# Zero padding moved from the K stacks to the Q stacks in a fused attention and GEGLU layer, with units reordered and new priorities

## The chip, the cores and the metric

One core of one Trainium2 chip runs the kernel. The metric is the device time of one launch in microseconds (us); the profile is of one execution of the same program. About 1% is what a timing of this kernel can tell from no change.

## The reference

One transformer layer over 2048 tokens of width 512, in fp32: pre-layer-norm attention with a compressive memory, then a pre-layer-norm GEGLU feed-forward, each with its residual.

```python
H = 32; Dh = 16; N = 4; L = 512              # heads, head width, segments, segment length
q, k, v = (split_heads(layernorm(x) @ w) for w in (wq, wk, wv))
for s in range(N):
    logits = qs @ ks.T * Dh ** -0.5 + mask   # causal inside the segment
    a_dot  = softmax(logits) @ vs
    pq     = phi(qs)                         # t + 1 where t > 0, else exp(t)
    a_mem  = (pq @ M) / (pq @ z + 1e-6)
    o      = g * a_mem + (1 - g) * a_dot     # g = sigmoid(beta), one per head
    M += phi(ks).T @ vs;  z += sum(phi(ks))
h  = x + concat(o) @ wo
h2 = h + (gelu(layernorm(h) @ w_gate) * (layernorm(h) @ w_up)) @ w_down   # 1376 hidden columns
```

## The kernel before

**Precision.** Most products are kept near fp32 by splitting operands into a high and a low fp32r part and adding three matmuls (high by high, high by low, low by high). For the attention logits the same three products sit in one matmul: a head's 16 dimensions are stacked four times in 64 partitions (high, low, high, and a row that carries a constant on the K side and the row maximum on the Q side). Two heads share the 128 partitions.

**Stacks.** Projections of q and k are written to `hl` tiles (high and low part, 128 partitions x 512 queries). Transfers issued by SP (L694 for Q, L700 for K) copy them, SBUF to SBUF, into the stacks `stq` and `stk`. Since two heads share the partitions, one operand must hold zeros where the other head lies. Before the change this is K: `stk` is `[128, 2, 2, 512]`, with one plane per head `a`, half of it zero, and `stq` is `[128, 2, 512]`.

**Units and halves.** The 32 heads are four chunks `c` of eight heads; a unit is a chunk in one segment `s` (`UNITS`, sixteen of them), and a half `Q` is four heads of a unit, two pairs `p` of two heads `a`. For each half:

- `pass_a` computes logits with queries as output rows (PE, L796), and DVE takes their negated masked row maxima with one reduction each (L806, `nm`). The maxima are split into high and low (L822, L825, `mm`), transposed (PE, L829), copied to `mx` (L832) and sent by a transfer into a free row of the Q stack (L834). Only keys up to the end of a block of 128 queries are computed.
- `pass_b` computes the logits again with keys as rows, in four key blocks `kb` of 128 (PE, L868, and L861 for `kb` 3), now with the maximum subtracted by the extra row. ACT takes exp (L875), GpSimd zeroes the upper triangle (L878), and `accum` multiplies by V with a column of ones for the sum (PE, L899, four heads side by side in 32-column tiles). For `kb` 3, GpSimd first adds the two K planes (`k3`, L846) and ACT spreads the Q stack over two planes (`q3`, L850), so that one matmul of 256 columns serves two heads.
- `mem` computes the memory part (L755, L771). `wo_seg` multiplies by `wo` (L972) and adds the residual; `ln2` normalizes (DVE, L561), transposes (PE, L578) and forms operands of the feed-forward, which is a Strassen-like product (`ffn`, L1144) and `down` (L1205).

**What sets the order.** The program is straight-line. A list scheduler (`Sched`) fixes the order of every engine's queue ahead of time: among the operations that could start within a small window of the earliest, it takes the one with the lowest priority number. A priority is the place in the program plus an offset from the table `DUE`, by kind of work (`q`, `k`, `d` for stack transfers, `v`, `m`, `a`, `b`, `p`, `o`, `w` for `wo`, `l` for the first layer norm) and by unit or half. Tiles come from pools (`Pool_`) that hand out buffers in order and pass them on to a later stage when they retire. The eight PSUM banks are three for projections and the like, two for `pass_a`, two for `pass_b`, one for `accum`.

Of the kernel before, what the change touches and what calls it, by code (L numbers as in the profile page):

```python
# [7 lines left out]
F32 = mybir.dt.float32  # L8
# [7 lines left out]
P = 128  # L16
# [12 lines left out]
UNITS = [(c, s) for h in range(2) for c in range(NCH) for s in (2 * h, 2 * h + 1)]  # L29
# [211 lines left out]
def infini_geglu(ctx: ExitStack, tc: tile.TileContext, x, wq, wk, wv, wo, beta,  # L241
# [56 lines left out]
    stk_t = many("stk", 4, [P, 2, 2, D], F32R)  # L298
    PSK = Pool_(stk_t, fifo=True, then=Parts(2, *[PBL] * 5, *[FIN] * 3))
    stq_t = slots("stq", 4)  # L300
    PSQ = Pool_(stq_t, fifo=True, then=Parts(1, PBL, PBL, Parts(2, *[PHH] * 2), Parts(2, *[PHH] * 2)))

    k3_t = many("k3", 1, [P, 2, P], F32R)
    q3_t = many("q3", 2, [P, 2, 2, P], F32R)
    PK3, PQ3 = Pool_(k3_t, fifo=True), Pool_(q3_t, fifo=True)
# [23 lines left out]
    PNM = Pool_(many("nm", 2, [P, 2, 2, 4]))  # L329
    PMM = Pool_(many("mm", 2, [P, 2, 2, 8], F32R))  # L330
    PMX = Pool_(many("mx", 2, [32, P]))
# [7 lines left out]
    one = sb("one", [P, 1])  # L339
    gt = sb("gt", [P, 2, NCH])  # L340
# [46 lines left out]
    vz3 = [Val() for _ in q3_t]  # L387
    vone, vq0, vk0, vv0 = Val(), [Val() for _ in stq_t], [Val() for _ in stk_t], [Val() for _ in va_t]

# [5 lines left out]
    def c_fill():  # L395
        for i, t in enumerate(stq_t):
            pool(0.93, -4.2 + 0.1 * i + (i > 1), lambda t=t: nc.gpsimd.memset(t.bitcast(F32), 0.0),
                 [vcalm[0]] if i > 1 else [], [vq0[i]])
        for i, t in enumerate(q3_t):
            pool(0.5, -3.8 + 0.1 * i, lambda t=t: nc.gpsimd.memset(t.bitcast(F32), 0.0),  # L400
                 [vcalm[0]], [vz3[i]])
        for i, t in enumerate(va_t):
            def ones(t=t):
                nc.gpsimd.memset(t[:, :, 16:136:17], 1.0)
                nc.gpsimd.memset(t[:, :, 136:152], 1.0)
            pool(0.25, -3.5 + 0.1 * i, ones, [vcalm[0]], [vv0[i]])

        def c_amask():
            nc.gpsimd.memset(amask, 0.0)
            nc.gpsimd.affine_select(amask[:, 3 * P:], amask[:, 3 * P:], pattern=[[-1, P]],  # L410
                                    compare_op=OP.is_ge, fill=NEG, base=0, channel_multiplier=1)
        pool(1.0, -3, c_amask, [vcalm[0]], [vamask])

    def c_stk(i, after):
        t = stk_t[i]
        for a in range(2):
            own, other = slice(64 * a, 64 * a + 64), slice(64 - 64 * a, 128 - 64 * a)
            act(2 * D, -4.2 + i, lambda a=a, own=own: nc.scalar.activation(
                t[own, :, a], one[own, :, None].to_broadcast([64, 2, D]), AF.Copy),
                [vone] + after, [vk0[i]], src=0.1, chain=True)  # L420
            pool(0.93, -4.2 + i, lambda a=a, other=other: nc.gpsimd.memset(
                t[other, :, a].bitcast(F32), 0.0), after, [vk0[i]], chain=True)


# [239 lines left out]
    def qkv(U):  # L664
# [8 lines left out]
        for i in range(2):  # L673
# [14 lines left out]
            for h, Q in enumerate(half):  # L688
                dst = (STQ, STK)[i][Q]
                zeros = (vq0, vk0)[i][Q:Q + 1]  # L690
                for r, part in enumerate(((0, 1, 0), (0, 0, 1))[i]):
                    if i == 0:
# [5 lines left out]
                    for a in range(2):  # L698
                        dma(moved + 0.2 + h, lambda dst=dst, r=r, part=part, h=h, hl=hl, a=a:
                            nc.sync.dma_start(  # L700
                                dst.t[64 * a + r:64 * a + 64:4, :, a].bitcast(F32),
                                hl.t[64 * h + 32 * a:64 * h + 32 * a + 32, part].bitcast(F32)),
                            [hl] + zeros, [dst], kb=64, chain=True)
                if i == 0 and Q >= len(stq_t):
                    dma(moved + 0.2 + h, lambda dst=dst: nc.sync.dma_start(
                        dst.t[3:P:32].bitcast(F32), amask[0:16, 0:2 * P]), [vamask], [dst],
                        kb=16, chain=True)
# [74 lines left out]
    def pass_a(Q):  # L782
# [4 lines left out]
        def part(heads, i):  # L787

            w = (i + 1) * P
# [513 lines left out]
```

## Time and profile before

| | us |
|---|---|
| median of three timed runs | 839.55 |
| lowest and highest | 834.55, 841.9 |
| span of the profiled execution | 837.1 |
| TensorE (PE) busy | 812.1 (97%) |
| VectorE (DVE) busy | 613.4 (73%) |
| ScalarE (ACT) busy | 540.6 (65%) |
| GpSimd (POOL) busy | 505.3 (60%) |
| TensorE matmuls | 4709 |

The span runs from the first to the last instruction of the profiled execution; its own launch time was not recorded apart, and the span lies inside the range of the timed runs. Busy time of PE includes modelled ends of pipelined matmuls, so an engine shown busy can still run below its pace. Attention fills the first 476 us or so, the feed-forward the rest.

### The profile page before, as it was taken

The numbers are of one execution on the slowest core, as the hardware profiler recorded it, in microseconds if no ns is written. First come the engines' busy times: TensorE is split into PE (matmuls) and PEld (weight loads), VectorE is DVE, ScalarE is ACT, GpSimd is POOL, SyncE is SP. The second block draws the span as 40 slices with busy tenths as digits, with TensorE's granted clock in tenths as the row PEclk, the third lists the DMA queues.
The fourth block names the chain that finished last, engine by engine and source line by source line (L and its number), as shares of the span: only waits on it lengthen the run. The fifth ranks groups of instructions, "written<-read, shape, count | busy, mean of one in ns | idle before, by whom it ended". The sixth has DMA issues, their size and how long they took to land.

```text
span 837.1 us, 15362 instructions
## 1 busy us (share of the span) xinstructions
PE 812.1 (97%) x4709; PEld 627.1 (75%) x4709; DVE 613.4 (73%) x1831; ACT 540.6 (65%) x1063; POOL 505.3 (60%) x751
## 2 busy tenths in 40 slices
PE   5999999999999999999999899999999999999998
PEld 4777787777767877677756588778788887788886
DVE  7888876797887887789686783677457956656565
ACT  6877778688876757776575662687467554545551
POOL 7534445544444645546755695788787676778750
PEclk9999999999999999999999799999999999999999
DMA  6643545636436554565554465531211251212102
GB/s 230 160 111 94 162 108 164 172 103 195 123 104 172 165 158 129 152 177 141 165 168 144 142 219 158 189 100 52 63 51 42 83 181 43 63 46 64 51 1 100
DMA packets 71750, 103.52 MB, mean 124 GB/s; under 512 B 14324, under 2 KB 24884, under 8 KB 71668
## 3 DMA queue, kind: packets, MB, share of 16 engines
q1 hardware_dynamic: 71668, 102.54, 42.1%
q8 instruction: 37, 0.61, 0.3%
q14 instruction: 45, 0.37, 0.1%
HBM read 54.92 MB, written 21.43 MB: 91 GB/s over the span
## 4 chain that ended last, share of the span: by engine, by line
PE 76%; DVE 11%; ACT 4%; DMA 3%; issue 3%; POOL 3%; SPq 1%; POOLq 0%; ACTq 0%; DVEq 0%
PE bank L1144 20%; PE bank L1205 13%; PE bank L899 8%; PE bank L796 7%; PE bank L618 7%; PE bank L868 6%; PE bank L972 5%; DVE junk L806 4%; PE bank L647 3%; PE bank L578 1%; POOL raw L1121 1%; PE bank L771 1%; PE bank L725 1%; DMA cd<-pv_dram 1%; DVE row L561 1%
## 5 line engine op out<-in xcount | busy, mean ns | idle before, releaser
L806 DVE CUSTOM_DVE_ANT_0 junk<-bank,amask 128x256 f32<-128x256 f32 (+3 forms) x512 | 228.2, 485 | 43.0 <-PE bank L796 39.4
L875 ACT ACTIVATE pt<-bank 128x512 f32<-128x512 f32 (+1 forms) x352 | 181.3, 559 | 53.9 <-PE bank L868 42.4
L878 POOL TENSOR_SCALAR_AFFINE_SELECT pt<-pt 128x128 f32<-128x128 f32 (+2 forms) x352 | 118.5, 347 | 155.3 <-ACT pt L875 151.0
L796 PE MATMUL bank<-stk,stq 128*128 128x512 f32 (+2 forms) x384 | 126.9, 377 | 3.7 <-DVE nm L806 2.1
L868 PE MATMUL bank<-stq,stk 128*128 128x384 f32 (+2 forms) x384 | 114.1, 356 | 2.9 <-ACT pt L875 2.3
L618 PE MATMUL bank<-xt,w 128*128 128x512 f32 x384 | 108.6, 395 | 1.2 <-DVE xt L588 1.1
L1210 DVE TENSOR_TENSOR pt<-pt,bank 128x512 f32<-128x512 f32 x96 | 64.9, 685 | 40.2 <-PE bank L1205 39.9
L796 PEld LDWEIGHTS bank<-stk,stq 128*128 128x128 f32 x384 | 68.4, 188 | 25.8 <-DVE nm L806 11.4
L868 PEld LDWEIGHTS bank<-stq,stk 128*128 128x128 f32 x384 | 67.1, 188 | 21.8 <-ACT pt L875 10.3
L618 PEld LDWEIGHTS bank<-xt,w 128*128 128x128 f32 x384 | 69.9, 188 | 12.6 <-DVE xt L588 1.6
L899 PE MATMUL bank<-pt,vaug 128*32 128x512 f32 (+3 forms) x1024 | 79.1, 445 | 0.0
L899 PEld LDWEIGHTS bank<-pt,vaug 128*32 128x32 f32 x1024 | 29.6, 111 | 41.0 <-issue 31.4
L647 PE MATMUL bank<-wv,xt 128*128 128x256 f32 x384 | 54.9, 283 | 0.1
L1144 PE MATMUL bank<-xt,w 128*128 128x512 f32 (+1 forms) x201 | 54.3, 391 | 0.0
L647 PEld LDWEIGHTS bank<-wv,xt 128*128 128x128 f32 x384 | 52.3, 190 | 2.2 <-DVE pq L630 0.4
L434 POOL TENSOR_TENSOR w<-raw,w 128x512 fp32r<-128x512 f32 x24 | 30.9, 1289 | 30.8 <-ACT w L429 27.6
L1114 POOL TENSOR_TENSOR w<-raw,w 128x512 fp32r<-128x512 f32 (+3 forms) x36 | 41.7, 1160 | 2.8 <-ACT w L1112 2.6
L1144 PEld LDWEIGHTS bank<-xt,w 128*128 128x128 f32 (+1 forms) x201 | 37.1, 186 | 8.3 <-ACT junk L1151 0.2
L806 DVE DVE_READ_ACCUMULATOR2_ANT nm<- 128x1 f32 x512 | 42.0, 82 | 0.0
L1144 PE MATMUL bank<-stk,w 128*128 128x512 f32 (+1 forms) x135 | 38.0, 390 | 0.3 <-DVE vaug L1156 0.3
L920 ACT ACTIVATE pvs<-bank 128x512 f32<-128x512 f32 x32 | 19.2, 599 | 28.6 <-PE bank L899 14.8
L1121 POOL TENSOR_TENSOR raw<-raw,raw 128x256 f32<-128x256 f32 (+1 forms) x44 | 35.8, 813 | 3.0
(299 smaller groups left out, 1805.5 us busy)
## 6 DMA issues: line engine op xcount, KB each, us to landing
stq<-hl SPq DMA_DIRECT2D x96, 128.0 KB
stk<-hl SPq DMA_DIRECT2D x192, 64.0 KB
pv_dram<-pvs SPq DMA_DIRECT2D x32, 256.0 KB
r<-r_dram SPq DMA_DIRECT2D x28, 256.0 KB
row<-x SPq DMA_DIRECT2D x24, 256.0 KB
raw<-wg SPq DMA_DIRECT2D x20, 256.0 KB
raw<-wu SPq DMA_DIRECT2D x20, 256.0 KB
raw<-wd SPq DMA_DIRECT2D x20, 256.0 KB
```

Source lines behind the costliest of these rows:

```text
L618: nc.tensor.matmul(pm.t, w.t[:, wi, dc * P:(dc + 1) * P], XT[s][dc].t[:, xi, :], start=dc == 0 and n == 0, stop=dc == ND - 1 and n == 2)
L647: nc.tensor.matmul(pm.t[:, 256 * t:256 * t + 256], XT[s][dc].t[:, xi, t0:t0 + P], whl[wi].t[:, h, 256 * (dc % 2):256 * (dc % 2) + 256], st ...
L796: nc.tensor.matmul(sa.t[:, k * w:(k + n) * w].rearrange("x (n w) -> x n w", n=n), sq.t[:, p, i * P:(i + 1) * P], sk.t[:, p, a:a + n, 0:w], ...
L806: nc.vector.tensor_tensor_reduce(out=junk.t[:, :w], in0=sa.t[:, k * w:(k + 1) * w], in1=amask[:, D - w:], op0=OP.add, op1=OP.min, scale=-1 ...
L868: nc.tensor.matmul(sc.t[:, lo:lo + D - q0], sk.t[:, p, a, q0:q0 + P], sq.t[:, p, q0:D], start=True, stop=True)
L875: act(w, prio, lambda: nc.scalar.activation(e.t[:, :w], sc.t[:, :w], AF.Exp), [sc], [e])
L878: nc.gpsimd.affine_select(v, v, pattern=pat + [[1, P]], compare_op=OP.is_ge, fill=0.0, base=0, channel_multiplier=-1)
L899: nc.tensor.matmul(pv.t[32 * n:32 * n + 32, kb * P:D], va.t[:, kb, 17 * j:17 * j + 32], e.t[:, lo:lo + D - kb * P], start=kb == 0, stop=la ...
L1121: pool(0.14 + 2.13e-3 * h, prio, lambda: nc.gpsimd.tensor_tensor(d.t[:, d0:d0 + h], a.t[:, a0:a0 + h], c.t[:, c0:c0 + h], op=o), ins, [d])
L1144: nc.tensor.matmul(dst.t[:w], v.t[:, wi, c0 + j * w:c0 + (j + 1) * w], b[bk][j].t[:, xi, :], start=first and j == 0 and n == 0, stop=j == ...
L1205: nc.tensor.matmul(pm.t, HH[p, f, s][hi].t[:w, t * P:(t + 1) * P], v.t[:w, wi, :], start=f == fl[0] and n == 0, stop=f == fl[-1] and n == 2)
L1210: dve(D, prio, lambda a=a, pm=pm: nc.vector.tensor_tensor(a.t, a.t, pm.t, op=OP.add), [pm], [a])
```

## The change

- **Stacks.** `stk` becomes `[128, 2, 512]`, with both heads filled. `stq` becomes `[128, 2, 2, 512]` and holds the zeros: for each block of 64 queries it has 64 columns of head 0 (zero in head 1's partitions) and then 64 columns of head 1. `planes` views it as blocks `i` (eight), head `a`, query `q`. The transfers into `stq` write runs of 64 queries; those into `stk` write whole rows.
- **Pass A.** A matmul takes 128 columns of the Q stack (two heads by 64 queries) against keys up to the end of the block of 64: widths 64, 128, ... 512. Two blocks share a bank (7 alone; 6 with 0, 5 with 1, 4 with 2; 3 of both pairs). The maxima of both heads lie in one row `nm`; a product with a 0/1 mask `own` (`ns`) puts them apart, and the split, transpose and transfer take twice the rows.
- **Pass B.** `k3` and `q3` are gone. For key blocks 2 and 3 one matmul covers both heads of a pair (512 and 256 columns).
- **Units.** `UNITS` takes two chunks of a segment together: (0,0), (1,0), (0,1), (1,1), (2,0), ... where it took (0,0), (0,1), (1,0), (1,1), ... Weight chunks are split two units ahead, and chunk 1's at the start.
- **Priorities.** `DUE` has new numbers, up to 5 in size where 4 was the limit, and new kinds: `w` by row block, `n` (second layer norm), `f`, `g`, `e` (feed-forward weights, products, down), `x`, `y` (weight chunks).

The diff, cut:

```diff
-UNITS = [(c, s) for h in range(2) for c in range(NCH) for s in (2 * h, 2 * h + 1)]
+UNITS = [(2 * g + c, s) for h in range(2) for g in range(2) for s in (2 * h, 2 * h + 1) for c in range(2)]
...
-    "w": [-3.5, -4, -2.375, 2],
+    "w": [3, -2.75, 3.375, -4, 3.25, -5, 4.875, -3.125, -2.875, -5, 5, 2.5, -4.125, 1.375, 2.75, 2],
+    "n": [1.125, 1, 2, 2.5],
...
-    stk_t = many("stk", 4, [P, 2, 2, D], F32R)
-    stq_t = slots("stq", 4)
-    k3_t = many("k3", 1, [P, 2, P], F32R)
-    q3_t = many("q3", 2, [P, 2, 2, P], F32R)
+    stk_t = slots("stk", 4)
+    stq_t = many("stq", 4, [P, 2, 2, D], F32R)
...
-    va_t = many("vaug", 6, [P, 4, 8 * 17 + 16])
+    va_t = many("vaug", 5, [P, 4, 8 * 17 + 16])
...
+    def planes(v):
+        return v.t.rearrange("x p b (i a q) -> x p (b i) a q", i=4, a=2)
...
                             nc.sync.dma_start(
-                                dst.t[64 * a + r:64 * a + 64:4, :, a].bitcast(F32),
+                                planes(dst)[64 * a + r:64 * a + 64:4, :, :, a].bitcast(F32),
                                 hl.t[64 * h + 32 * a:64 * h + 32 * a + 32, part].bitcast(F32)),
...
-                        n = 2 if i < 2 else 1
-                        nc.tensor.matmul(
-                            sa.t[:, k * w:(k + n) * w].rearrange("x (n w) -> x n w", n=n),
-                            sq.t[:, p, i * P:(i + 1) * P], sk.t[:, p, a:a + n, 0:w],
-                            start=True, stop=True)
+                for (p, i), lo in zip(parts, at):
+                    w = 64 * (i + 1)
+                    nc.tensor.matmul(sa.t[:, lo:lo + w], planes(sq)[:, p, i].rearrange("x a q -> x (a q)"),
+                                     sk.t[:, p, 0:w], start=True, stop=True)
...
-        for i in (3, 2):
-            for n in range(4):
-                part([(n % 2, n // 2)], i)
-        for p in range(2):
-            part([(0, p), (1, p)], 1)
-        part([(0, 0), (1, 0), (0, 1), (1, 1)], 0)
+        for i in (7, 6, 5, 4):
+            for p in range(2):
+                bank([(p, i), (p, 6 - i)] if i < 7 else [(p, i)])
+        bank([(0, 3), (1, 3)])
...
+            nc.vector.tensor_tensor(ns.t, nm.t[:, None, :].to_broadcast([P, 2, 16]),
+                                    own[:, :, None].to_broadcast([P, 2, 16]), op=OP.mult)
...
-        pool(0.69, prio, lambda: nc.gpsimd.tensor_tensor(
-            k3.t, sk.t[:, :, 0, 3 * P:].bitcast(F32), sk.t[:, :, 1, 3 * P:].bitcast(F32), op=OP.add), [sk], [k3])
-        for a in range(2):
-            own = slice(64 * a, 64 * a + 64)
-            act(2 * P, prio, lambda a=a, own=own: nc.scalar.activation(
-                q3.t[own, :, a], sq.t[own, :, 3 * P:], AF.Copy), [sq, mr] + zeros, [q3], src=0.22, chain=True)
...
+                    k = sk.t[:, p, q0:q0 + P]
+                    if kb < 2:
+                        nc.tensor.matmul(sc.t[:, lo:lo + D - q0].rearrange("x (i q) -> x i q", q=64), k, planes(sq)[:, p, 2 * kb:, parts[0][0] % 2],
+                                         start=True, stop=True)
+                    else:
+                        nc.tensor.matmul(
+                            sc.t[:, lo:lo + 2 * (D - q0)].rearrange("x (a i q) -> x a i q", a=2, q=64),
+                            k, planes(sq)[:, p, 2 * kb:].rearrange("x i a q -> x a i q"), start=True, stop=True)
...
+    for i in range(2):
+        W[0, 1, i] = split_weight(2 + (-3.175) + DUE["x"][1], (wq, wk)[i][1], PW, after=[vcalm[0]])
```

**Where instructions move: pass A on TensorE.** These are rows of TensorE's queue in the first half's pass A: operation, output bank, the two operands, shape, and how often in a row. Before, with projections of the next unit (L618) between:

```order
L618 MATMUL bank_66<-xt_77,w_81 128x512 x3
L796 MATMUL bank_69<-stk_87,stq_91 128x512
L618 MATMUL bank_66<-xt_78,w_81 128x512 x3
L618 MATMUL bank_65<-xt_77,w_82 128x512 x3
L796 MATMUL bank_68<-stk_87,stq_91 128x512
L618 MATMUL bank_66<-xt_79,w_81 128x512 x3
L796 MATMUL bank_69<-stk_87,stq_91 128x384
```

Of the change (L808 is the matmul of pass A now, L739 the memory update, L632 the projection):

```order
L808 MATMUL bank_69<-stk_87,stq_91 128x448
L808 MATMUL bank_69<-stk_87,stq_91 128x64
L808 MATMUL bank_68<-stk_87,stq_91 128x448
L808 MATMUL bank_68<-stk_87,stq_91 128x64
L739 MATMUL bank_66<-vaug_132,pkn_122 128x136 x4
L808 MATMUL bank_69<-stk_87,stq_91 128x384
L808 MATMUL bank_69<-stk_87,stq_91 128x128
L632 MATMUL bank_67<-xt_73,w_84 128x512 x3
```

Where a bank held one matmul of 384 or 512 columns, it now holds a wide and a narrow one that fill it to 512, and a half has 16 matmuls for 12.

**The queue of transfers.** SP's rows for the first unit's stacks, before (destination, source, partitions x rows x run length):

```order
L694 DMA stq_91<-hl_98 32x2x512 x3
L700 DMA stk_87<-hl_99 16x2x512 x6
L694 DMA stq_92<-hl_98 32x2x512 x3
L700 DMA stk_88<-hl_99 16x2x512 x6
L1057 DMA gt<-beta 128x1x4
```

and of the change:

```order
L714 DMA stq_91<-hl_95 16x16x64 x6
L708 DMA stk_87<-hl_96 32x2x512 x3
L714 DMA stq_92<-hl_95 16x16x64 x6
L708 DMA stk_88<-hl_96 32x2x512 x3
L442 DMA raw_103<-wk 128x512
```

There are nine issues a half in both; the long list of short runs has moved from the K to the Q stack.

**The seam between attention and feed-forward on TensorE.** Before, from the last product with `wo` that the second layer norm needs (L972) over the last half's pass B (L868, L861) to the first transposes (L578):

```order
L972 MATMUL bank_67<-wv_86,wv_85 128x512 x3
L868 MATMUL bank_71<-stq_94,stk_90 128x512
...
L868 MATMUL bank_70<-stq_94,stk_90 128x384
L861 MATMUL bank_71<-q_97,k_95 128x256 x2
L868 MATMUL bank_70<-stq_94,stk_90 128x256 x2
L868 MATMUL bank_71<-stq_94,stk_90 128x256 x2
L1144 MATMUL bank_70<-xt_76,hl_100 128x512 x3
L578 MATMUL bank_65<-ident,row_104 128x128
```

Of the change (L973 the product with `wo`, L900 P times V of the half before, L592 the transposes):

```order
L973 MATMUL bank_66<-w_82,wv_85 128x512 x3
L900 MATMUL bank_72<-pt_106,vaug_132 32x512
...
L868 MATMUL bank_70<-stq_93,stk_89 128x384
L592 MATMUL bank_65<-ident,row_101 128x128
...
L868 MATMUL bank_71<-stq_93,stk_89 128x384
L592 MATMUL bank_67<-ident,row_101 128x128
```

The sixteen P times V matmuls of the half before now stand behind that product, where they stood ahead of it, and the first transposes stand before the last five matmuls of pass B.

More of the change, by code (lines that the diff above doesn't have):

```diff
@@ L339, in infini_geglu @@
     one = sb("one", [P, 1])
+    own = sb("own", [P, 2])
     gt = sb("gt", [P, 2, NCH])
@@ L409, in c_amask @@
             nc.gpsimd.memset(amask, 0.0)
-            nc.gpsimd.affine_select(amask[:, 3 * P:], amask[:, 3 * P:], pattern=[[-1, P]],
-                                    compare_op=OP.is_ge, fill=NEG, base=0, channel_multiplier=1)
+            for a in range(2):
+                v = amask[64 * a:64 * a + 64, D - 64:]
+                nc.gpsimd.affine_select(v, v, pattern=[[-1, 64]], compare_op=OP.is_ge, fill=NEG,
+                                        base=0, channel_multiplier=1)
         pool(1.0, -3, c_amask, [vcalm[0]], [vamask])
@@ L415, in c_stk @@
         t = stk_t[i]
-        for a in range(2):
[L417 to L422, printed above, removed]
+        act(2 * D, -4.2 + i, lambda: nc.scalar.activation(
+            t, one[:, :, None].to_broadcast([P, 2, D]), AF.Copy), [vone] + after, [vk0[i]], src=0.1)
+        for p in range(2):
+            pool(0.93, -4.2 + i, lambda p=p: nc.gpsimd.memset(
+                stq_t[i][:, p].bitcast(F32), 0.0), after, [vq0[i]], chain=True)
+    def planes(v):
+        return v.t.rearrange("x p b (i a q) -> x p (b i) a q", i=4, a=2)
     def split_weight(prio, src, pool_, w=D, rows=P, lo="POOL", after=(), early=3.0):
```

126 lines of the change are left out of this document (57 added, 69 removed), and 41 rows, old and new, of the table DUE.

## The prediction

> **What bounds the kernel now.** I read the head of the page first, then the table of windows, cut where the character of the work changes (the columns after the window are its length, then the busy us of PE, PE's weight loads, DVE, ACT and POOL with their instruction counts, the granted clock, the DMA share, GB/s).
>
> ```profile
> span 837.1 us, 15362 instructions
> PE 812.1 (97%) x4709; PEld 627.1 (75%) x4709; DVE 613.4 (73%) x1831; ACT 540.6 (65%) x1063; POOL 505.3 (60%) x751
> PE 76%; DVE 11%; ACT 4%; DMA 3%; issue 3%; POOL 3%; SPq 1%; POOLq 0%; ACTq 0%; DVEq 0%
> 0.00:20.00 20.00, 11.41 (x60) 9.08 (x61) 15.28 (x44) 12.56 (x19) 14.03 (x35) 1.00 0.70 236
> 20.00:60.00 40.00, 38.74 (x261) 31.32 (x260) 35.35 (x136) 30.54 (x65) 19.39 (x31) 1.00 0.52 137
> 60.00:200.00 140.00, 138.95 (x1008) 105.70 (x1005) 110.18 (x445) 105.68 (x217) 69.07 (x150) 1.00 0.51 139
> 200.00:260.00 60.00, 57.02 (x400) 42.01 (x398) 50.12 (x207) 45.49 (x96) 24.45 (x54) 1.00 0.48 131
> 260.00:420.00 160.00, 158.66 (x1125) 118.85 (x1123) 126.18 (x496) 112.05 (x230) 89.13 (x181) 1.00 0.56 157
> 420.00:440.00 20.00, 18.25 (x113) 11.57 (x117) 17.89 (x63) 14.56 (x29) 11.54 (x23) 1.00 0.53 164
> 458.00:480.00 22.00, 18.93 (x85) 10.84 (x86) 16.63 (x28) 13.36 (x26) 13.01 (x19) 0.77 0.45 143
> 480.00:837.00 357.00, 352.17 (x1555) 285.26 (x1554) 231.06 (x378) 196.56 (x367) 253.49 (x243) 1.00 0.29 89
> ```
>
> TensorE sets the time: it is busy for 97% of the span and 76% of the chain that ended last. So a change counts by two things: the TensorE work that it adds or removes, and how much of TensorE's 25.0 us of idle time (837.1 - 812.1) it gives back. The windows say where that idle time lies: 8.6 us in the first 20 us, 1.3 in the next 40, 1.1 in 60 to 200, 3.0 in 200 to 260, 1.3 in 260 to 420, 1.8 in 420 to 440, 3.1 in 458 to 480, and 4.8 after that. In 458 to 480 the granted clock is 0.77 as well, which is another 0.23 x 22 = 5.1 us. The change rewrites the attention stage (up to about 476 us); the feed-forward stage behind it is nearly without gaps and keeps its matmuls.
>
> **The prices on TensorE.** In the chain of work that ended last, unbroken rows give the pace of a matmul (start, us, line, count).
>
> ```profile
> 820.97 12.25 PE bank L1205 x54
> 107.21 0.72 PE bank L647 x6
> 636.87 0.87 PE bank L578 x8
> 61.08 0.86 PE bank L771 x2
> ```
>
> 512 columns cost 12.25 / 54 = 0.227 us; 256 columns cost 0.72 / 6 = 0.120. The line through both gives 0.200 for 448, 0.173 for 384 and 0.147 for 320. L578 is a 128-column transpose at 0.87 / 8 = 0.109. L771 is a plain fp32 product of 512 columns, which runs as two matmuls and costs 0.86 in all, 1.68 ns a column against the 0.42 of the line. No row shows what the change adds: fp32r matmuls of 64, 128 and 192 columns. The weight loads give a lower bound.
>
> ```profile
> L796 PEld LDWEIGHTS bank<-stk,stq 128*128 128x128 f32 x384 | 68.4, 188 | 25.8 <-DVE nm L806 11.4
> L899 PEld LDWEIGHTS bank<-pt,vaug 128*32 128x32 f32 x1024 | 29.6, 111 | 41.0 <-issue 31.4
> ```
>
> Loading 128 columns takes 188 ns, 32 columns 111 ns: (188 - 111) / 96 = 0.80 ns a column, 103 ns for 128. Every matmul with a stationary operand of its own needs that load, so a short one costs no less than 0.103; I take 0.109, the nearest short row. The upper end is the fp32 price, 1.68 ns a column: 0.107, 0.215 and 0.322 for 64, 128 and 192 columns.
>
> A rule of the Trainium skill would make them cheaper: TensorE: Matmul & The Clock Gate, section "Back-to-back issue gap", gives about 81 ns a matmul for a stream of load and matmul pairs at 128 columns. By it the 192 short matmuls would cost 28 ns less each, 5.4 us in all, and the forecast would be 827.4, inside its own range; no run here shows such a pace, and the load rows above stand against it.
>
> **The change, part by part.** All of it is per half (4 heads of a chunk in one segment), and there are 32 halves.
>
> *Pass A (L796) on TensorE.* Before, 4 matmuls of 512, 4 of 384, 2 of 512 and 2 of 256: 6 x 0.227 + 4 x 0.173 + 2 x 0.120 = 2.29 us. After, for each of two pairs of heads, eight matmuls from 64 to 512 columns: 2 x (0.227 + 0.200 + 0.173 + 0.147 + 0.120 + 3 x 0.109) = 2.39 us. There are 10% fewer columns (4608 for 5120), but four more matmuls at the floor: +0.10 us, +3.0 us over 32 halves (up to +23.5 at the fp32 price: 2 x (0.106 + 0.213) x 32 = 20.4 more).
>
> *Pass B (L868) on TensorE.* The four matmuls of 256 columns for the third key block become two of 512: 2 x 0.227 - 4 x 0.120 = -0.026, or -0.8 us. The last block keeps two of 256. Together TensorE gains **2.2 us of work**, all on the bound.
>
> *VectorE.* The masked minima shrink with the columns.
>
> ```profile
> L806 DVE CUSTOM_DVE_ANT_0 junk<-bank,amask 128x512 f32<-128x512 f32 x128 | 85.4, 684 | 17.8 <-PE bank L796 16.9
> L806 DVE CUSTOM_DVE_ANT_0 junk<-bank,amask 128x128 f32<-128x128 f32 x128 | 29.9, 285 | 3.0 <-PE bank L796 2.9
> L825 DVE TENSOR_TENSOR mm<-nm,mm 128x16 fp32r<-128x16 f32 x32 | 7.0, 220 | 0.4
> ```
>
> (684 - 285) / 384 = 1.04 ns a column and 152 ns fixed; 16 reductions before and after, 512 columns fewer: -0.53 us a half. The added product with the mask `own` is small, like L825: +0.22 to 0.25; two operands grow by 16 columns (+0.03). Net -0.26, -8 us of 613, in the engine that is fullest beside TensorE in the attention stage (110.18 of 140 us).
>
> *ScalarE and GpSimd.* The copies into `q3` and `k3` go, and with them two steps ahead of pass B's last key block.
>
> ```profile
> L850 ACT ACTIVATE q<-stq 64x256 fp32r<-64x256 f32 x64 | 26.4, 412 | 6.7 <-DMA stq<-mx 6.0
> L846 POOL TENSOR_TENSOR k<-stk 128x256 fp32r<-128x256 f32 x32 | 23.6, 738 | 11.1 <-PE bank L861 7.6 <-POOL pt L878 1.6 <-PE bank L829 0.7
> ```
>
> ScalarE loses 26.4 us of work and a place where its in-order queue stood still for the row maxima (6.0 us); GpSimd loses 23.6. Of the fills at the start, GpSimd's on the Q stacks go from four to eight, and its eight half-fills of K stacks go; ScalarE's fills go from eight to four. All of this lies beside TensorE, so it counts only where TensorE waits for these engines. If that cover were not there, nothing would be lost: work only goes.
>
> *The queue of transfers.* The 96 copies into Q stacks and 192 into K stacks become 192 and 96: as many issues. But the Q stack is now written in runs of 64 queries, 256 B, where runs were 2 KB: 192 transfers of 16 x 16 runs are 49152 packets, in place of 6144.
>
> ```profile
> DMA packets 71750, 103.52 MB, mean 124 GB/s; under 512 B 14324, under 2 KB 24884, under 8 KB 71668
> q1 hardware_dynamic: 71668, 102.54, 42.1%
> L694 SPq DMA_DIRECT2D stq<-hl x96: 537/588/1390, 20.0 to 415.2; - x96
> L700 SPq DMA_DIRECT2D stk<-hl x192: 534/590/1612, 22.0 to 432.7; - x192
> ```
>
> A mean packet (102.54 MB / 71668 = 1431 B) takes 0.421 x 16 x 837.1 / 71668 = 79 ns. A 256 B packet costs between its share of the bytes, 14 ns (then nothing is added), and a whole mean packet, 79 ns (49152 x 79 / 16 = 242 us of every DMA engine, less 43 for the 6144 it replaces). I take the lower end as nearer, since the transfer moves the same bytes. Issuing costs SP 0.588 us at 64 runs and 0.590 at 32, so I put 256 runs at the same 0.59.
>
> The Trainium skill has a rule against this edit: DMA: Bandwidth & Descriptors, section "Specifications", puts the smallest transfer for full rate at 512 B; its section "Why small descriptors are slow (HBM only)" exempts SBUF to SBUF copies, which these are. By the first the second rival below would come true, by the second the sum stands; no packet of 256 B is in this trace.
>
> **What the new order gives back.** The priorities decide it, and the rows of the order show two places. The largest is the seam between attention and feed-forward.
>
> ```profile
> 455.68 2.29 PE bank L899 x32
> 457.97 0.91 PE bank L972 x3
> 465.27 3.96 DVE row L561 x4
> 469.27 2.18 PE bank L578 x9
> 471.45 4.27 PE bank L899 x32
> 475.73 0.60 PE bank L578 x4
> ```
>
> After the last product with `wo` (L972, 457.97) VectorE needs until 469.23 for the layer norm, TensorE has 14 matmuls for it, and the last P times V then runs at the low clock: 4.27 us for what took 2.29. The new order puts the P times V of the half before (2.3 us) behind that last product, so 2.3 us of work fills the hole and the clock may hold (2.0 us): I take **-4 us** (0 to -8.2, the window's whole idle and clock loss). In 420 to 440 the sixteen transposes of the other layer norm now stand in groups of four between pass A and pass B, not twelve in a row: **-1** (0 to -1.8). In 200 to 260 and the rest of attention VectorE and ScalarE release banks sooner:
>
> ```profile
> PEld bank L796 <- DVE nm L806: 11.4, 30, 1.3
> PEld bank L868 <- ACT pt L875: 10.3, 28, 0.9
> PE bank L496 <- DVE bn L490: 7.5, 1, 7.5
> ```
>
> Weight loads wait 21.7 us for them, mostly behind running matmuls; of the 3.0 us idle in 200 to 260 I take back 2, of the rest **1**, so **-3** (0 to -5.4, with the idle time of the two windows beside it). At the start the first 7.5 us are fixed by the load of `x` and its statistics; a second unit that needs only segment 0's inputs fills a little more: **-1** (0 to -2.4).
>
> **Sum.** 837.1 + 2.2 - 4 - 1 - 3 - 1 = 830.3 us of span. That span is of one profiled execution; the three timed runs (834.55 to 841.9) have a median 2.45 above it. So 830.3 + 2.45 = 832.8. With the recoveries halved or all but exhausted the same case gives 827 to 838.
>
> **The rivals.**
> 1. *Short fp32r matmuls are paid like fp32* (the slower side). Place: the 128- and 192-column matmuls of pass A, four in each half; price 20.4 us, on the bound, so 832.8 + 20.4 = 853. It ends slower than before once it eats the 6.8 us gained, at a third of that excess. For it: every fp32r matmul of this trace has 256 columns or more. Against it: the pace from 512 down to 256 is one straight line, and the load gives a floor below it.
> 2. *The 256 B packets fill the DMA engines.* At 79 ns each engine gets 199 us more within some 460, and the attention stage's share goes from about 0.52 to 0.95. Stacks arrive late; DMA's 3% of the chain (25 us) grows with the share, by 0.43 / 0.52 at the worst, 21 us; half to three quarters of it gives 843 to 849, say 848. It decides from about 40 ns a packet.
> 3. *The change does not free what TensorE waits for.* The new order has new holes in place of the old, and only the added work remains: 837.1 + 2.2 + 2.45 = 841.7. For it: 260 to 420 has 1.3 us idle in 160, so there is little to win in most of attention.
> 4. *The order closes nearly all holes.* Of 25.0 us idle, 7.5 at the start and the 3.9 of the last transfer behind 833.2 (820.97 + 12.25) stay; 13.6 and the clock's 5.1 go: 837.1 + 2.2 - 18.7 + 2.45 = 823, or 818 with back-pressure that now hides in busy time.
>
> **How the numbers follow.** Forecast 0.42, rival 1 0.15, rival 2 0.08, rival 3 0.18, rival 4 0.17. One per cent, about what a measurement of this kernel tells from no change, is 831.2 and 847.9. Faster: rival 4 and 0.45 of the forecast's own range (827 to 838), 0.36. Slower: rival 1 and half of rival 2, 0.19. Within: 0.45. The range reaches from rival 4's lower value, 818, to rival 1's, 854; beyond lie 0.04 below and about 0.08 above.
>
> **What would show it.** TensorE should count 4709 + 128 - 64 = 4773 matmuls; 64- to 192-column matmuls should start 0.10 to 0.11 us apart (rival 1: 0.21 and 0.32). ScalarE should lose 26 to 30 us, GpSimd 23 to 28, the minima 17. DMA share in 60 to 420 should stay below 0.6 (rival 2: above 0.8). The window around the seam should show a clock above 0.9 if -4 holds. I am wrong if the windows of 60 to 200 and 260 to 420, now 2.4 us idle in 300, open up, or if the start grows, where two more weight chunks are split early.

## The result, and the profile after

The changed kernel took 832.59 us in the median of 13 runs (829.55 to 835.1), the kernel before 839.55 us beside it on the same chip: ratio 0.9922, 95% interval 0.9900 to 0.9943. In a second session it was 830.87 against 838.38, ratio 0.9916 (0.9891 to 0.9942). The forecast was 832.8. The span of its profiled execution is 830.1 us, 7.0 less than before; forecast was 830.3. Not every place from which its sum took the gain gave it, though, as the parts below show.

The head of the page after, its chain, two rows on transfers, and the stretches of the table of windows that were shown of before (length, busy us of PE, weight loads, DVE, ACT, POOL with counts, granted clock, DMA share, GB/s):

```profile
span 830.1 us, 15398 instructions
PE 805.7 (97%) x4773; PEld 635.1 (77%) x4773; DVE 598.7 (72%) x1863; ACT 510.9 (62%) x995; POOL 478.0 (58%) x716
PE 84%; DVE 8%; ACT 2%; DMA 2%; issue 1%; POOL 1%; SPq 1%; ACTq 0%; DVEq 0%
DMA packets 116229, 104.49 MB, mean 126 GB/s; under 512 B 63476, under 2 KB 75508, under 8 KB 116148
q1 hardware_dynamic: 116148, 103.52, 45.2%
```

```profile
0.00:20.00 20.00, 11.14 (x53) 9.01 (x54) 14.76 (x41) 10.29 (x15) 11.47 (x36) 1.00 0.68 233
20.00:60.00 40.00, 37.67 (x235) 33.75 (x237) 34.40 (x146) 23.49 (x55) 12.26 (x19) 0.96 0.47 110
60.00:200.00 140.00, 139.44 (x1059) 106.89 (x1052) 107.59 (x462) 102.94 (x209) 65.50 (x143) 1.00 0.57 147
200.00:260.00 60.00, 59.14 (x435) 45.80 (x434) 49.12 (x209) 43.66 (x89) 22.07 (x56) 1.00 0.61 158
260.00:420.00 160.00, 155.75 (x1117) 117.33 (x1115) 119.33 (x489) 99.13 (x198) 82.42 (x163) 1.00 0.58 151
420.00:440.00 20.00, 17.62 (x113) 12.11 (x113) 19.27 (x68) 10.91 (x22) 8.16 (x17) 1.00 0.69 195
458.00:480.00 22.00, 20.96 (x132) 14.28 (x132) 17.80 (x36) 16.98 (x34) 17.98 (x23) 0.92 0.63 199
480.00:830.00 350.00, 346.14 (x1537) 282.70 (x1535) 223.45 (x370) 192.02 (x360) 247.62 (x240) 1.00 0.29 88
```

TensorE's time splits into busy time, idle time and what a low clock costs (length x missing share of the clock):

| us | before | after | forecast |
|---|---|---|---|
| idle and clock, 0 to 20 | 8.6 | 8.9 | |
| 20 to 60 | 1.3 | 2.3 + 1.6 | start in all: -1 |
| 60 to 200, 200 to 260 | 1.1, 3.0 | 0.6, 0.9 | |
| 260 to 420 | 1.3 | 4.3 | 60 to 420 in all: -3 |
| 420 to 440 | 1.8 | 2.4 | -1 |
| 458 to 480 | 3.1 + 5.1 | 1.0 + 1.8 | -4 |
| 480 to the end | 4.8 | 3.9 | 0 |
| idle and clock in all | 30.1 | 27.8 | -9 |
| busy time less the clock's part | 807.0 | 802.3 | +2.2, all work |
| span | 837.1 | 830.1 | -6.8 |

So 2.3 us came from holes and clock, where nine were expected, and 4.7 us from busy time, where 2.2 more were expected. Busy time is not work alone, however. A matmul of 512 columns is recorded as 0.42 us long on average, while the next one usually starts 0.23 us after it, so a short wait between two starts shows as busy:

```profile
L808 PE MATMUL bank<-stk,stq 128*128 128x512 f32 x64 | 25.3, 421 | 2.2 <-DVE nm L816 1.3 <-DVE mb L748 0.8
```

The run with the copies put back (below) has the same matmuls, and its busy time less the clock's part is 806.4 us, 4.1 more. Work has to be read from the starts of matmuls. By them it rose by 2 to 3 us (pass A by 3.0, as worked out below; pass B, forecast at -0.8, wasn't measured apart). So the waits and the clock's loss fell by 9 to 10 us in all, and some 7 of these lay inside the busy time. The experiments ask for the causes.

### The profile page after: what moved, and what is told of

Same layout as the page of the kernel before. It is cut to its first block, busy times and chain, and to the rows that moved or that the text cites. A ratio compares the mean times of both kernels' runs of the same rounds, so it can differ in the third digit from the quotient of the medians.

```text
span 830.1 us, 15398 instructions
## 1 busy us (share of the span) xinstructions
PE 805.7 (97%) x4773; PEld 635.1 (77%) x4773; DVE 598.7 (72%) x1863; ACT 510.9 (62%) x995; POOL 478.0 (58%) x716
## 4 chain that ended last, share of the span: by engine, by line
PE 84%; DVE 8%; ACT 2%; DMA 2%; issue 1%; POOL 1%; SPq 1%; ACTq 0%; DVEq 0%
PE bank L1147 24%; PE bank L1208 14%; PE bank L632 9%; PE bank L808 8%; PE bank L900 7%; PE bank L868 6%; PE bank L661 5%; PE bank L973 4%; PE bank L871 2%; DVE junk L816 2%; PE bank L739 1%; PE bank L785 1%; PE bank L592 1%; DMA cd<-pv_dram 1%; PE bank L731 1%
## 5 line engine op out<-in xcount | busy, mean ns | idle before, releaser
L816 DVE CUSTOM_DVE_ANT_0 junk<-bank,amask 128x448 f32<-128x448 f32 (+7 forms) x512 | 212.0, 453 | 40.4 <-PE bank L808 38.4
L876 ACT ACTIVATE pt<-bank 128x512 f32<-128x512 f32 (+1 forms) x352 | 182.6, 560 | 55.3 <-PE bank L868 32.7
L808 PE MATMUL bank<-stk,stq 128*128 128x448 f32 (+7 forms) x512 | 113.6, 312 | 4.5 <-DVE nm L816 3.6
L632 PE MATMUL bank<-xt,w 128*128 128x512 f32 x384 | 110.8, 402 | 1.1 <-DVE xt L602 1.1
L808 PEld LDWEIGHTS bank<-stk,stq 128*128 128x128 f32 x512 | 87.3, 189 | 23.2 <-DVE nm L816 9.2
L868 PE MATMUL bank<-stq,stk 128*128 128x512 f32 (+1 forms) x256 | 89.4, 396 | 2.5 <-ACT pt L876 1.2
L900 PE MATMUL bank<-pt,vaug 128*32 128x512 f32 (+3 forms) x1024 | 76.9, 435 | 0.0
L632 PEld LDWEIGHTS bank<-xt,w 128*128 128x128 f32 x384 | 67.0, 188 | 10.9 <-DVE xt L602 1.3
L900 PEld LDWEIGHTS bank<-pt,vaug 128*32 128x32 f32 x1024 | 29.1, 109 | 40.4 <-issue 30.6
L868 PEld LDWEIGHTS bank<-stq,stk 128*128 128x128 f32 x256 | 45.2, 189 | 18.8 <-issue 5.7
L661 PE MATMUL bank<-wv,xt 128*128 128x256 f32 x384 | 57.9, 289 | 0.0
L661 PEld LDWEIGHTS bank<-wv,xt 128*128 128x128 f32 x384 | 52.6, 192 | 2.0
L448 POOL TENSOR_TENSOR w<-raw,w 128x512 fp32r<-128x512 f32 (+1 forms) x27 | 34.9, 1292 | 32.6 <-ACT w L443 28.2
L1147 PE MATMUL bank<-xt,w 128*128 128x512 f32 (+1 forms) x156 | 42.6, 391 | 0.0
L816 DVE DVE_READ_ACCUMULATOR2_ANT nm<- 128x1 f32 x512 | 42.2, 82 | 0.0
L1117 POOL TENSOR_TENSOR w<-raw,w 128x512 fp32r<-128x512 f32 (+2 forms) x30 | 33.8, 1128 | 12.8 <-ACT w L1115 12.8
L871 PE MATMUL bank<-stq,stk 128*128 128x512 f32 (+1 forms) x128 | 38.0, 361 | 0.0
L1117 POOL TENSOR_TENSOR stq<-raw,stq 128x512 fp32r<-128x512 f32 (+2 forms) x28 | 32.4, 1158 | 9.5 <-ACT stq L1115 8.7
L1147 PE MATMUL bank<-xt,stq 128*128 128x512 f32 (+1 forms) x135 | 37.1, 392 | 0.0
```

The source lines that it names most:

```text
L632: nc.tensor.matmul(pm.t, w.t[:, wi, dc * P:(dc + 1) * P], XT[s][dc].t[:, xi, :], start=dc == 0 and n == 0, stop=dc == ND - 1 and n == 2)
L661: nc.tensor.matmul(pm.t[:, 256 * t:256 * t + 256], XT[s][dc].t[:, xi, t0:t0 + P], whl[wi].t[:, h, 256 * (dc % 2):256 * (dc % 2) + 256], st ...
L808: nc.tensor.matmul(sa.t[:, lo:lo + w], planes(sq)[:, p, i].rearrange("x a q -> x (a q)"), sk.t[:, p, 0:w], start=True, stop=True)
L816: nc.vector.tensor_tensor_reduce(out=junk.t[:, :w], in0=sa.t[:, lo:lo + w], in1=amask[:, D - w:], op0=OP.add, op1=OP.min, scale=-1.0, scal ...
L868: nc.tensor.matmul(sc.t[:, lo:lo + D - q0].rearrange("x (i q) -> x i q", q=64), k, planes(sq)[:, p, 2 * kb:, parts[0][0] % 2], start=True, ...
L876: act(w, prio, lambda: nc.scalar.activation(e.t[:, :w], sc.t[:, :w], AF.Exp), [sc], [e])
```

## The experiments

### What a short matmul costs

In the trace after, medians from a short matmul's start to the next start are 0.029 us at 64 columns, 0.060 at 128, 0.089 at 192. So a pair of a wide matmul and its narrow one takes 0.24 us, as 512 columns do. But the matmul behind the pair takes longer than it does behind a wide one: at the medians of its width by 0.081 us behind 64 columns, 0.053 behind 128 and 0.023 behind 192. Together a short one costs 0.11 us at each of the three widths. The chain of the trace after shows three pairs (384 + 128, 320 + 192 and 448 + 64 columns), and around the last one six products with `wv`, ahead of it and behind it:

```profile
115.38 0.24 PE bank L808 x2
117.03 0.24 PE bank L808 x2
```

```profile
124.20 0.72 PE bank L661 x6
124.92 0.24 PE bank L808 x2
125.16 0.79 PE bank L661 x6
```

The first run issues each short one three times:

```diff
                     w = 64 * (i + 1)
-                    nc.tensor.matmul(sa.t[:, lo:lo + w], planes(sq)[:, p, i]...
+                    for _ in range(3 if i < 3 else 1):
+                        nc.tensor.matmul(sa.t[:, lo:lo + w], planes(sq)[:, p, i]...
```

> The changed kernel, with each pass A matmul of 64, 128 and 192 columns issued three times in a row with the same operands (384 more matmuls, 128 of each width; same scores). In the trace of the changed kernel a matmul of 64, 128 or 192 columns is followed by the next one after 0.029, 0.060 and 0.089 us in the median. Theory A, a short matmul costs its columns and no more: 128 x (0.029 + 0.060 + 0.089) = +22.8 us, about 855. Theory B, the weight load is a floor of 0.103 us that a wide neighbour hid, so that a short matmul behind a short one pays it: +384 x 0.103 = +39.6 us, about 872. If TensorE's time was not the bound there, less than +15.

Measured: 865.33 us, ratio to before 1.0339 (1.0297 to 1.0380), 32.7 us above the changed kernel. Its chain, with one wide matmul and three short ones in each piece (448 + 3 x 64, 384 + 3 x 128, 320 + 3 x 192):

```profile
120.97 0.46 PE bank L809 x4
122.20 0.46 PE bank L809 x4
124.36 0.46 PE bank L809 x4
```

Two more short matmuls cost 0.22 us, 0.110 each, whether they have 64, 128 or 192 columns. The time lies between the two theories. Theory B has the price right: a short matmul has a floor, and 0.110 is near the 0.103 that the forecast took from the weight loads. That the load is this floor is argued from the two numbers. 384 x 0.110 = 42 us, of which 33 show: TensorE's busy time grew by 38.5 us, and its idle time fell by 5.4 (24.4 to 19.0). What theory B says of the wide neighbour, that it hides the floor, doesn't hold: the matmul behind the short one pays what is missing, as the 0.79 above shows.

The rule in the Trainium skill that fits this is not the one that the prediction weighed. TensorE: Matmul & The Clock Gate, section "LDWEIGHTS (loading the stationary operand)", gives columns / 1.2 ns for a load, 107 ns for 128; the 0.110 us agrees. The 81 ns of "Back-to-back issue gap" was not met: 128 columns cost 0.11 us beside a wide matmul and behind a short one.

The counterpart leaves the short matmuls out:

```diff
                 for (p, i), lo in zip(parts, at):
+                    if i < 3:
+                        continue
```

> The changed kernel without the matmuls of 64, 128 and 192 columns of pass A (192 of them; their minima are taken over columns of the wide matmul in the same bank, as many as before, so those row maxima are of other scores). VectorE's work and the order stay. Theory: beside a wide matmul a short one costs its columns, 64 x (0.029 + 0.060 + 0.089) = 11.4 us of TensorE, of which 8 to 11 show (822 to 825). The price put on them in the forecast, 0.109 each, would give 20.9 us (about 812). If the minima on VectorE set the pace of pass A, 0 to 4 us.

Measured: 825.69 us, ratio 0.9842 (0.9813 to 0.9872) where the changed kernel in the same session has 0.9916: 6 us less, below the 8 to 11 of the theory. TensorE's busy time fell by 10.6 us (805.7 to 795.1), which looks like the columns' 11.4. The chain says otherwise. At the place shown above, a wide matmul and the six products behind it took 1.03 us with the short one between them (0.24 + 0.79); without it they take 0.92, again 0.11 less:

```profile
123.91 0.20 PE bank L810
124.11 0.71 PE bank L661 x6
124.83 0.18 PE bank L810
```

So the 192 short ones took about 21 us, the price in the forecast, and some 15 of these came back as waits, part of them inside the busy time. TensorE's idle time grew by 3.7 us (24.4 to 28.1), and the weight loads of pass A waited 10.6 us longer for the minima (`nm`), whose work stayed. Weight loads of pass A, after and without the short ones:

```profile
L808 PEld LDWEIGHTS bank<-stk,stq 128*128 128x128 f32 x512 | 87.3, 189 | 23.2 <-DVE nm L816 9.2 <-issue 3.4 <-DVE mb L748 0.9
```

```profile
L810 PEld LDWEIGHTS bank<-stk,stq 128*128 128x128 f32 x320 | 58.1, 190 | 30.1 <-DVE nm L818 19.8 <-issue 3.2 <-DVE pk L644 0.4
```

### Packets of 256 B

```diff
-  planes(dst)[64 * a + r:64 * a + 64:4, :, :, a].bitcast(F32),
+  dst.t[64 * a + r:64 * a + 64:4, :, a].bitcast(F32),
```

> The changed kernel, with the rows of the Q stacks written in runs of 512 queries (2 KB) in place of 64 (256 B); the heads are then not interleaved in the stack, so the scores belong to other queries. 6144 packets in place of 49152, same bytes, same number of issues, same order. Theory: the 256 B packets cost the kernel nothing, same time within 1% (830 to 835), DMA share in 60 to 420 lower by less than 0.05. Rival: they hold stacks back; then 3 to 10 us faster, and the DMA share falls by 0.1 or more.

Measured: 830.67 us, ratio 0.9920 (0.9892 to 0.9948), the same as the changed kernel's 0.9922. Its row of the queue:

```profile
q1 hardware_dynamic: 73140, 103.52, 43.3%
```

43008 packets fewer take (0.452 x 830.1 - 0.433 x 829.0) x 16 = 259 us off all the engines together. That is 6 ns a packet on top of the time for its bytes, which the prediction put at 14.

### Relief of ScalarE and GpSimd, from both sides

Into the changed kernel the removed amount of work is put back, on ScalarE ahead of the exponentials and on GpSimd ahead of the mask:

```diff
+                if kb == 3:
+                    for a in range(2):
+                        r = slice(64 * a, 64 * a + 64)
+                        nc.scalar.activation(spare[r, 0], one[r, :, None].to_broadcast([64, 2, P]), AF.Copy)
...
+                if kb == 3:
+                    nc.gpsimd.tensor_tensor(spare[:, 1], amask[:, 0:2 * P]..., amask[:, P:3 * P]..., op=OP.add)
```

> The changed kernel, with work of the kind and amount that was removed put back where it stood, without its waits: ahead of the exponentials of each half's last key block two copies of 64x256 on ScalarE (about 26 us in all), ahead of their mask a sum of 128x256 on GpSimd (about 24 us). They write a spare tile that nobody reads. Theory: the relief of these two engines gave nothing, since TensorE lost 6.4 of the 7.0 us by work of its own; 0 to +2 us. Rival: the relief gave the banks back sooner and is part of the gain: +3 to +7 us, with more idle time of TensorE behind the exponentials.

Measured: 838.96 us, ratio 1.0023 (1.0002 to 1.0044), against 0.9922: the rival was right, and the whole gain is gone. Its span is 836.4, 6.3 more than after. The window in which most new idle time lies (TensorE 3.4 us idle, after 0.6):

```profile
60.00:200.00 140.00, 136.60 (x1006) 104.47 (x999) 105.30 (x450) 107.86 (x222) 71.86 (x153) 1.00 0.54 144
```

The waits show what the relief acts on. Weight loads of pass B wait for the exponentials (`pt`): 11.4 us before (the 10.3 of L868 that the prediction shows, and the first row here; us in total, times, longest), 7.2 after (the next two) and 18.2 in this run (the last two):

```profile
PEld bank L861 <- ACT pt L875: 1.1, 2, 0.7
PEld bank L868 <- ACT pt L876: 5.4, 16, 1.0
PEld bank L871 <- ACT pt L876: 1.8, 7, 0.5
PEld bank L869 <- ACT pt L882: 5.5, 16, 1.0
PEld bank L872 <- ACT pt L882: 12.7, 23, 1.2
```

Work put into an order made without it might cost more than the same work taken away gains; so the kernel before was run without its copies:

```diff
-        pool(0.69, prio, lambda: nc.gpsimd.tensor_tensor(k3.t, ...), [sk], [k3])
+        pool(0.69, prio, lambda: None, [sk], [k3])
...
-            act(2 * P, prio, lambda a=a, own=own: nc.scalar.activation(q3.t[own, :, a], ...), ...)
+            act(2 * P, prio, lambda a=a, own=own: None, ...)
...
-                            k3.t[:, p], q3.t[:, p], start=True, stop=True)
+                            sk.t[:, p, 0, 3 * P:], sq.t[:, p, None, 3 * P:].to_broadcast([P, 2, P]), ...)
```

> The kernel before, with the copies into q3 (ScalarE) and k3 (GpSimd) left out and the order of everything else kept; pass B's last key block reads the stacks instead, so the second head of a pair gets the first head's scores there. This takes away the same 26.4 us of ScalarE and 23.6 us of GpSimd that the change removes, and the wait of ScalarE for the row maxima. Theory: if their relief is a gain of its own, as the 6 us lost by giving it back suggest, 3 to 7 us faster than before (832 to 836). Rival: an order made for one set of durations loses by any work that is put in and gains nothing by work that is taken away; within 1.5 us of before.

Measured: 833.83 us against 838.79, ratio 0.9939 (0.9915 to 0.9964): 5 us, in the order of before. The relief is a gain of its own, close to what the whole change brings. In this profile, of the fastest of its five executions, most of what shows as idle time and clock lies at the seam, 3.4 us where the kernel before lost 8.2 (3.1 idle at a clock of 0.77):

```profile
458.00:480.00 22.00, 21.72 (x111) 15.54 (x112) 20.24 (x36) 16.48 (x31) 17.86 (x23) 0.86 0.63 213
```

### Relief of VectorE

```diff
-  out=junk.t[:, :w], in0=sa.t[:, k * w:(k + 1) * w], in1=amask[:, D - w:],
+  out=junk.t[:, :w - 32], in0=sa.t[:, k * w:(k + 1) * w - 32], in1=amask[:, D - w:D - 32],
```

> The kernel before, with every masked minimum of pass A taken over 32 columns fewer (the last 32 of each block are left out of the row maxima): 16 x 32 = 512 columns a half at 1.04 ns, 17 us of VectorE in all, what the change takes off it; TensorE's work and the order are kept. Theory: TensorE waits for these minima (11.4 us in its weight loads), so their shortening gives 1 to 4 us. Rival: nothing within 1.5 us, since the waits lie behind running matmuls.

Measured: 836.92 us against 838.79, ratio 0.9985 (0.9965 to 1.0005). The interval reaches from 3 us of gain to nothing; this doesn't decide.

### The late priorities and the seam

```diff
+for kind in "nfge":
+    DUE[kind] = [0] * len(DUE[kind])
```

> The changed kernel with four of the new kinds of priorities set to zero (n, f, g, e: the second layer norm, and weights, products and down projections of the feed-forward stage), as they were before; the rest as changed. Theory: they closed the seam between attention and feed-forward (3.1 us idle and a clock of 0.77 before, 1.0 us and 0.92 after), so the seam opens again: +3 to +6 us, all behind 420. Rival: the seam is closed by the order of attention; 0 to +1.5 us.

Measured: 837.46 us, ratio 1.0010 (0.9988 to 1.0033) against 0.9922; the span is 834.8, 4.7 us more. The seam has 4.5 us idle where the changed kernel has 1.0, and 260 to 420 has 6.1 where it has 4.3:

```profile
260.00:420.00 160.00, 153.91 (x1101) 114.56 (x1099) 120.03 (x476) 97.16 (x193) 81.95 (x159) 1.00 0.57 149
458.00:480.00 22.00, 17.54 (x93) 11.66 (x93) 18.26 (x36) 14.83 (x30) 15.13 (x20) 0.92 0.56 182
```

The theory holds for the seam, and without the new priorities of the later stage nothing is left of the gain. But not all of the loss lies behind 420, as was expected.

### Where it was given back: a hole and the clock

By these runs, relief and priorities are each worth 5 to 6 us, together more than the 7.0 of the whole change. They overlap in part, since each of them narrows the seam, and part was given back. The table says where: 20 to 60 and 260 to 420, 5.6 us in all. TensorE's timeline after, from 25 us (start, length, line, count, in brackets the idle time and its releaser), and the chain's pieces ahead of the hole:

```profile
26.76 0.87 PE L661 MATMUL bank<-wv,xt 128*128 128x256 f32 x6
29.86 0.66 PE L731 MATMUL bank<-ident,pk 128*128 128x128 f32 x4 [2.24 <-DVE pk L644]
30.28 1.24 PE L661 MATMUL bank<-wv,xt 128*128 128x256 f32 x6
```

```profile
25.75 3.46 DVE pt L546 x4
29.21 0.61 DVE pk L644
29.86 0.66 PE bank L731 x4
```

The transposes of the first unit's phi(K) (L731) wait for VectorE, which first normalizes segment 1's rows (L546, 3.46 us). The products with `wv` (L661) behind them need nothing new. Then the clock falls:

```profile
28.00:30.00 2.00, 0.14 (x1) 0.14 (x2) 2.00 (x7) 0.00 (x0) 0.18 (x1) 1.00 0.79 178
30.00:32.00 2.00, 2.00 (x14) 2.00 (x14) 0.56 (x2) 1.91 (x5) 0.00 (x0) 0.69 0.57 121
32.00:34.00 2.00, 2.00 (x11) 2.00 (x10) 0.87 (x3) 1.30 (x3) 0.00 (x0) 0.50 0.47 99
34.00:36.00 2.00, 2.00 (x16) 1.92 (x15) 1.22 (x3) 1.08 (x2) 0.00 (x0) 0.96 0.83 187
```

The run with late priorities at zero has the same order up to here and the same hole, and there the clock stays:

```profile
28.65 0.66 PE L735 MATMUL bank<-ident,pk 128*128 128x128 f32 x4 [2.24 <-DVE pk L648]
```

```profile
30.00:32.00 2.00, 2.00 (x18) 1.91 (x16) 0.91 (x3) 2.00 (x7) 0.00 (x0) 1.00 0.48 102
32.00:34.00 2.00, 1.89 (x16) 1.60 (x14) 2.00 (x6) 1.65 (x6) 0.00 (x0) 1.00 0.64 142
```

So it is a matter of the single execution. The next runs fill the hole, and then three more, by moving what is issued, not what is computed:

```diff
+        ahead, done = {90: (91,), 114: (92,)}, set()
...
-            o.fn()
+            if o.idx == 113:
+                emit(self.ops[76])
+            emit(o)
+            for i in ahead.get(o.idx, ()):
+                emit(self.ops[i])
```

Operation 76 is phi(K) of the first unit, 113 the normalization of segment 1's rows, 91 and 92 are six products with `wv` each, and 114 is a group of segment 1's transposes. The run with four holes has three more such pairs.

> The changed kernel with three operations moved at one place (the rest of the order word for word the same): in the trace of the changed kernel TensorE stands still from 27.6 to 29.9 us, since the transposes of the first unit's phi(K) come ahead of products with wv that need nothing new, and phi(K) itself comes on VectorE behind the normalization of segment 1's rows (3.46 us); then the granted clock is 0.5 for 4 us. Here phi(K) stands ahead of that normalization, and 12 products with wv stand earlier. Theory: this hole with its clock is where the change loses what it gains elsewhere: the hole falls below 1 us, the clock of 20 to 60 us returns to 1.00, and the time falls by 2 to 4 us (828.5 to 830.5). Rival: VectorE sets the pace up to 60 us, and the wait appears again behind it: within 1 us of 832.6.

> As the run with the first hole filled, and in three more places (holes of 1.31, 1.03 and 0.85 us at 291, 348 and 433 us of the changed kernel's trace) one triple of ready products moved ahead of the matmul that waits there. Theory: each of these waits is a matter of what stands next in TensorE's queue; 2 to 3 us less than the run with the first hole filled (826 to 828). Rival: the triple is missing where it stood before, and the wait moves there: within 1 us of it.

Measured: 829.19 us, ratio 0.9907 (0.9877 to 0.9936), and 828.48 us, ratio 0.9888 (0.9862 to 0.9915). In the first the hole is 0.49 us and the clock of 20 to 60 is 1.00:

```profile
29.03 0.66 PE L602 MATMUL bank<-ident,pt 128*128 128x128 f32 x4 [0.49 <-DVE hl L705]
```

```profile
20.00:60.00 40.00, 38.82 (x272) 32.93 (x271) 33.77 (x146) 25.14 (x57) 11.91 (x20) 1.00 0.49 113
```

The step from one hole to four is within both intervals and decides nothing. Since the intervals overlap the changed kernel's, it was run again beside the one with four holes filled:

> The changed kernel again, beside the two runs with holes filled, on one chip: 831 to 834, with a clock below 1 after the hole at 28 us in some of its runs and not in others (its runs so far have mean clocks of 0.994 to 0.999 and spans of 827.5 to 832.8).

> The kernel with four holes filled, beside the changed kernel on the same chip: 3 to 5 us less than it (827 to 829) if the holes and the clock behind the first are what it loses; rival, 1.5 us or less, if other waits take their place.

Measured: 830.87 us, ratio 0.9916 (0.9891 to 0.9942), and 828.84 us, ratio 0.9888 (0.9864 to 0.9912): 2 us, between what theory and rival said. The intervals overlap a little, but the 0.9888 came twice. So a gain of this size is likely, not settled. This version is the fastest of those that compute the whole layer, 1.1% under the kernel before. Some executions of the changed kernel have a mean clock of 0.999, which leaves no room for the drop behind the hole; so its median holds only part of the 3.8 us by which the profiled spans of the run with one hole filled and of the changed kernel differ (826.3 and 830.1).

## Why the prediction was right, and where it was wrong

The time is right to 0.2 us, and the case is the forecast's: faster by the relief of the engines beside TensorE and by the seam, with a little more work on TensorE. That the sum under it hits so closely is in part luck: the holes gave back too little, and waits that it put at nothing made up for it.

*TensorE's work, +2.2 forecast.* That "a short one costs no less than 0.103; I take 0.109" was right: it is 0.110 in the run with three of each, 0.11 with the matmul behind in the trace after. At the medians of both traces behind a wide matmul, and with these prices, pass A went from 74.8 us in all halves to 77.8, +3.0; the forecast was +3.0. Whoever reads only the 0.029 us from a short matmul to the next start takes it for nearly free.

*What the new order gives back, -9 forecast, -2.3 measured.* The seam's -4 came a little larger (8.2 to 2.8), with the clock above 0.9 as said, and the run without the priorities shows that they hold it closed. They are one of two causes: in the order of before, the relief alone took 4.8 us off there, which the prediction didn't ask. In 200 to 260 the idle time fell by 2.1, as said. The other places went the other way, and both were named as what would make the forecast wrong: 260 to 420 opened by 2.9 us, and the start to 60 us grew by 2.9. There the prediction put -1 on a second unit that "fills a little more"; it did not ask what that unit's rows stand behind on VectorE. The hole follows from the order of VectorE's queue, which could have been read before.

*What the sum put at nothing: waits inside the busy time, some 7 us.* The prediction saw that weight loads wait "mostly behind running matmuls" and took back 3 us for all of it. Only its fourth rival counted "back-pressure that now hides in busy time". The rows of the waits for the exponentials show where the relief works on them; which waits make up the whole isn't shown.

*The costs beside TensorE.* ScalarE lost 29.7 us and GpSimd 27.3, inside the bounds given; the minima 16.5 for 17 (64 times the means of the eight shapes, 231.9 us, against 248.4). The first and the last of these shapes, and the added product:

```profile
L816 DVE CUSTOM_DVE_ANT_0 junk<-bank,amask 128x512 f32<-128x512 f32 x64 | 43.4, 686 | 9.2 <-PE bank L808 9.1
L816 DVE CUSTOM_DVE_ANT_0 junk<-bank,amask 128x64 f32<-128x64 f32 x64 | 13.9, 217 | 0.0
L830 DVE TENSOR_TENSOR ns<-nm,own 128x32 f32<-128x32 f32 x32 | 7.9, 246 | 0.4
```

That this relief counts through earlier banks was right in kind, as the waits for the exponentials show, and too low in size: 3 us were put on earlier banks in 60 to 420, while the relief gives 5 in the order of before, the seam with it. The packets came near the lower end.

*The rivals.* The first is out: a short matmul costs 0.11. The second is out: some 20 ns a packet (14 + 6), where it needed 40, and the DMA share in 60 to 420 is 0.58. The third is half true: what was freed in one place came back in others. The fourth asked for the holes that are still there.

What stays open is why 260 to 420 opened. Two of its largest holes end with VectorE's minima (L816), as the timeline after has it:

```profile
291.89 0.50 PE L808 MATMUL bank<-stk,stq 128*128 128x512 f32 x1 [1.31 <-DVE nm L816]
414.57 0.50 PE L808 MATMUL bank<-stk,stq 128*128 128x384 f32 x2 [1.03 <-DVE nm L816]
```

Whether the order of the units, the priorities or the longer tail of pass A brings these late isn't shown: no run changes the layout alone or the order of the units alone.

## What to carry to other kernels

Price a short matmul with a stationary operand of its own at a floor, here 0.11 us for 64 to 192 columns, also beside a wide one; and read its cost up to the end of the matmul behind it, since part of it shows only there. Don't take busy time for work: compare runs with the same matmuls, or read the starts. In a queue that is served in order, ask for each waiting instruction whether the one behind it could have gone first: here 12 ready products stood behind one wait of 2.24 us. And when a forecast comes true, check its terms: here the holes gave back 7 us too little, waits inside the busy time gave back some 7 that nobody had counted, and the total hid both.

## What the hardware showed beside that

A hole of 2.24 us was enough to halve TensorE's clock for 3.4 us in the profiled execution after (the three windows from 30 to 36 us lack 1.7 us of clock in all), and the same hole in another run left it at 1.00. The Trainium skill (TensorE: Matmul & The Clock Gate, section "What's actually happening") has a free-running window of 3413 ns behind the clock, which fits a drop that comes and goes; its "after ≥1 idle window (~3.4µs)" is longer than the 2.24 us measured here.
